# Batch 0's values pair by pair, an earlier request for w_in, and six units ahead of batch 1's scores

## The chip, the cores and the metric

The kernel runs on one core of a Trainium2 chip. The metric is device time in microseconds (us); the kernel before took 324.68 us, the median of three runs (324.43 to 324.69). Lower is better.

A core has a matrix engine (TensorE, PE in the profile, with its weight loads as PEld), three engines for elementwise work (VectorE or DVE, ScalarE or ACT, GpSimd or POOL) and SyncE (SP), which here only issues transfers. Each engine works through its own list of instructions in order; semaphores tie them together. ACT and POOL issue some transfers too.

## The reference

Attention over a sliding window with a linear bias by distance, and then a two-layer block on its output, in float32:

```python
scores = scale * np.matmul(q, k.transpose(0, 1, 3, 2))     # q, k, v: 8 batches, 8 heads, 576, 64
bias = slopes[:, None, None] * (-np.abs(rel))[None]
mask = (rel >= 0) & (rel < 128)
scores = np.where(mask, scores + bias[None], -1000000000.0)
attn = softmax(scores)                                      # over the last axis
x = np.matmul(attn, v).transpose(0, 2, 1, 3).reshape(4608, 512)
h = x @ w_in                                                # w_in: 512 x 2048
g = h * np.clip(h + 3.0, 0.0, 6.0) / 6.0
out = g @ w_out                                             # w_out: 2048 x 512
```

## The kernel before

**Tiling.** Heads go in pairs: pair g = 4·b + hp holds heads 2·hp and 2·hp+1 of batch b, so pairs 0 to 3 are batch 0, 4 to 7 batch 1, and so on to 31. The 576 positions are five blocks of 128 (the last has 64). For a pair, `scores_diag` multiplies each block of q with its own block of k and `scores_off` with the block before; `exp_diag`, `exp_off` and `exp_full` are ScalarE's exponentials, whose results wait in rooms of `w_out_sb` (batch 0) and `gbuf[1]` (batch 1). `attend`, `attend_split` or `values` multiply them with v (in `vbuf`, with a column of ones that yields the sums), and DVE divides into `avs`. `back` transposes `avs` on PE, and a copy puts the result into `xT`, the input of the second part. For pair 3 ScalarE copies the left part of `xT` (L475) and DVE the right part (L476).

**The second part.** Rows go in tiles of 512. `moe_up(nt, ms)`, a *unit* in this document, makes 128 of the 2048 hidden columns for tile nt: four matmuls (L492, one for each pair's quarter of `xT`), a ScalarE activation (L516) and a DVE multiplication (L517). Units 0 to 3 of tile 0 read w_in's first quarter, 4 to 7 the second, and so on. `up_begin` and `up_more` do the first matmuls of a unit when only some pairs are ready. `moe_down` multiplies with w_out. `fill(n)` puts the next n units or quarter-steps of `moe_down` into the engines' lists, unless the batch that they need isn't done.

**Loads.** q and k of the first batches come in four transfers each through `load_double` (two pairs at once, L98), are cast by `prepare_double` (L239, on DVE or GpSimd as the call says), transposed by nine PE transposes in a score bank and copied into `qTb` and `kTb` by `wide_double` (L282, L284). The first two pairs of batch 0 come by `load_run` (L92). v comes by `load_block` (L110): one block of 128 positions for all heads, five blocks for a batch, cast into `vbuf` by `cast_v` (L193). w_in's first quarter is loaded in float32 into `raw`, a part of `gbuf[0]` (L177), and cast by `cast_raw` (L180), one of its four pieces at a time. The other quarters come through GpSimd's own queue with a cast on the way, `load_w_in` (L169); `second_w_in` asks for the second and is held back by a one-element memset of `w_out_sb` until pair 1's exponentials in that room have been read.

**Order.** No scheduler moves anything: `manual_schedule` keeps the order of the calls as written. `first_batch` does batch 0, the start of the units and the preparation of batch 1's q and k; `second_batch` does batch 1's scores with units between; from pair 8 on `segment` repeats a fixed pattern. The PSUM banks are two wide score buffers ("sc"), two "h", one "av" and one "o"; a unit of tile 0 takes an "h" bank, but units 2, 8 and 12 take "av" and units 5 and 11 "o". A tile waits until the last reader of its bank is done.

Of the kernel before, what the change touches and what calls it, by code (L numbers as in the profile page):

```python
# [10 lines left out]
FP32 = mybir.dt.float32  # L11
BF16 = mybir.dt.bfloat16
# [6 lines left out]
def kernel(  # L19
# [88 lines left out]
    def load_block(b, nm, j, eng):  # L108
        n = min(128, S - j * 128)
        eng.dma_start(out=tokens(b, nm)[:n, j, :, :],  # L110
                      in_=src_of[nm][b, :, ds(j * 128, n), :].rearrange("h p d -> p h d"))

    def load_tokens(b, nm):
        for j in range(NQ):
            load_block(b, nm, j, nc.sync)
# [24 lines left out]
    def memsets():  # L140
        nc.gpsimd.memset(vbuf[0][:, :, :, D:W], 1.0)
        nc.gpsimd.memset(vbuf[0][64:128, 4, :, 0:D], 0.0)

    def memsets_later():
        for i in range(2):
            nc.gpsimd.memset(p4buf[i], 1.0)
        nc.gpsimd.memset(kTb[1][:, :, 4, LAST:128], 0.0)
        nc.gpsimd.memset(vbuf[1][:, :, :, D:W], 1.0)
        nc.gpsimd.memset(vbuf[1][64:128, 4, :, 0:D], 0.0)
        nc.gpsimd.memset(tbuf[64:128, :, 4, :], 0.0)  # L150

    def warm_up(n):
# [38 lines left out]
    def cast_v(b, j, copy):  # L191
        n = min(128, S - j * 128)
        copy(out=vbuf[b % 2][:n, j, :, 0:D], in_=ld[b, "v"][:n, j, :, :])  # L193

    def cast_tokens(b, nm):
        s = ld[b, nm]
# [72 lines left out]
    def double_copy(b, dp, nm, i, copies):  # L269
        dst = (qTb if nm == "q" else kTb)[b % 2][:, 2 * dp + i, :, :]  # L270
        for part, (t0, t1) in enumerate(((0, 5), (5, RT))):
            copies[part](out=dst.rearrange("p j c -> p (j c)")[:, 0:S].rearrange(
                             "p (a t) -> p a t", t=RT)[:, :, t0:t1],
                         in_=st[b, dp, nm, part].rearrange("p t (a i) -> p i a t", i=2)[:, i])
# [38 lines left out]
    def scores_diag(g):  # L313
        rooms(g)
        b, hp = divmod(g, NP)
        qT, kT = qTb[b % 2][:, hp, :, :], kTb[b % 2][:, hp, :, :]
        first = not diag_tabled(g)
        if (g, "scd") not in st:
            tables_diag(g)
        scd = st[g, "scd"]  # L320
        for j in range(4):
            for e in range(2):
                r = slice(e * D, (e + 1) * D)
                nc.tensor.matmul(scd[:, e, ts(j, 128)], lhsT=kT[r, j, :],  # L324
                                 rhs=qT[r, j, :], start=first, stop=first or j == 3)
# [40 lines left out]
    def exp_full(g):  # L366
        for e in range(2):
            exp_diag(g, e)
        exp_off_full(g)
# [89 lines left out]
    def by_xbar(g):  # L459
        return g >= XB and g not in (XB + 2, XB + 3)  # L460

    def back(g, tag=None):
        b, hp = divmod(g, NP)
        avs = st[g, "avs"].rearrange("p j e d -> p j (e d)")
        if by_xbar(g):
            nc.sync.dma_start_transpose(
                out=xT[:, hp, ds(b % 4 * S, SP)].rearrange("p (j c) -> p j c", j=NQ),
                in_=avs.rearrange("p j c -> p (j c)"))
            return
        tag = tag or ("o" if b < 2 else "h")  # L470
        tp = BANKS[tag].tile([128, SP], BF16, tag=tag, name="tb", padded_shape=[128, 1024])
        for j in range(NQ):
            nc.tensor.transpose(tp[:, ts(j, 128)], avs[:, j, :], ident)
        if g == NP - 1:
            nc.scalar.copy(out=xT[:, hp, ds(b % 4 * S, 256)], in_=tp[:, 0:256])  # L475
            nc.vector.tensor_copy(out=xT[:, hp, ds(b % 4 * S + 256, S - 256)], in_=tp[:, 256:S])  # L476
            return
        eng = nc.vector.tensor_copy if g == 2 * NP - 1 else nc.scalar.copy
        eng(out=xT[:, hp, ds(b % 4 * S, S)], in_=tp[:, 0:S])  # L479
# [123 lines left out]

    def first_batch():
        prepare(0, (V, A))
        load_block(0, "v", 1, nc.scalar)
        for j in (4, 0, 2, 3):
            load_block(0, "v", j, nc.sync)
        load_raw()
        warm_up(5)  # L610
        tables_diag(0)
        tables_off(0)
        transposes(0, (V, A))
        scores_diag(0)
        prepare(1, (P, V))
        transposes(1, (V, V))
        scores_off(0)
        exp_full(0)
        scores_diag(1)
        prepare_double(0, 1, (V, P), "qk")  # L620
        tables_off(1)
        scores_off(1)
        double_begin(0, 1, "q", ("av", "o"))
        double_begin(0, 1, "k", ("h", "h"))
        exp_full(1)
        double_copy(0, 1, "q", 0, (V, V))
        double_copy(0, 1, "k", 0, (A, A))
        scores_diag(2)
        double_copy(0, 1, "q", 1, (V, V))
        double_copy(0, 1, "k", 1, (V, V))  # L630
        tables_off(2)
        scores_off(2)
        exp_full(2)
        scores_diag(3)
        cast_v(0, 4, P)
        cast_v(0, 0, P)
        cast_v(0, 1, P)
        cast_v(0, 2, V)
        cast_v(0, 3, V)
        scores_off(3)  # L640
        exp_full(3)
        attend(0)
        for dp in range(2):
            for nm in "kq":
                load_double(1, dp, nm, nc.sync)
        load_tokens(1, "v")
        attend_split(1, ("av", "h"))
        attend(2)
        back(0, "o")
        cast_raw(0, P)  # L650
        cast_raw(1, P)
        attend(3)
        cast_raw(2, A)
        back(1, "av")
        cast_raw(3, P)
        prepare_double(1, 0, (P,), "k")
        second_w_in()
        up_begin(0, 0, 1)
        up_begin(0, 1, 1)
        back(2, "o")  # L660
        prepare_double(1, 0, (V,), "q")
        up_more(0, 0, 2)
        up_more(0, 1, 2)
        back(3, "av")
        wide_double(1, 0, "k", V)
        wide_double(1, 0, "q", A)
        up_more(0, 0, 3)
        up_more(0, 1, 3)
        done[0] = NP
        fill(2)  # L670
        prepare_double(1, 1, (P,), "k")
        load_w_in(2)
        prepare_double(1, 1, (P,), "q")
        load_w_in(3)
        for dp in range(2):
            for nm in "kq":
                load_double(2, dp, nm, nc.sync)

    def second_batch():
        scores_diag(NP + 0)  # L680
        exp_diag(NP + 0, 0)
        exp_diag(NP + 0, 1)
        fill(2)
        scores_off(NP + 0)
        exp_off_full(NP + 0)
        wide_double(1, 1, "k", V)
        fill(1)
        wide_double(1, 1, "q", V)
        fill(1)
        scores_diag(NP + 1)  # L690
        exp_diag(NP + 1, 0)
        exp_diag(NP + 1, 1)
        fill(2)
        scores_off(NP + 1)
        exp_off_full(NP + 1)
        fill(1)
        cast_tokens(1, "v")
        scores_diag(NP + 2)
        exp_diag(NP + 2, 0)
        exp_diag(NP + 2, 1)  # L700
        fill(1)
        scores_off(NP + 2)
        exp_off_full(NP + 2)
        fill(2)
        for i in range(0, 4):
            load_w_out(i)
        g = 2 * NP - 1
        scores(g)
        exp_diag(g, 0)
        exp_diag(g, 1)  # L710
        prepare_double(2, 0, (V, P))
        prepare_double(2, 1, (P, P))
        nc.gpsimd.memset(ldbuf[2][:, 0:1], 0.0)
        load_tokens(2, "v")
        for dp in range(2):
            load_double(3, dp, "k", nc.sync)
        load_tokens(3, "q")
        exp_off_full(g)
        fill(1)
        attend(NP)  # L720
        fill(1)
        attend(NP + 1)
        fill(1)
        back(NP)
        attend(NP + 2)
        fill(1)
        back(NP + 1)
        double(2, 0, "k", 0, "av", A)
        attend(NP + 3)
        back(NP + 2)  # L730
        double(2, 0, "k", 1, "av", A)
        wide_double(2, 0, "q", A)
        up_begin(1, 0, 3)
        back(2 * NP - 1)
        up_begin(1, 1, 3)
        done[0] = 2 * NP
        fill(2)
        scores_diag(2 * NP)
        scores_off(2 * NP)
# [50 lines left out]
    with tc.manual_schedule(engines=every):  # L790
        load_run(0, "k", nc.scalar)
        load_run(0, "q", nc.sync)
        load_run(1, "k", nc.scalar)
        load_run(1, "q", nc.sync)
        load_double(0, 1, "k", nc.scalar)
        load_double(0, 1, "q", nc.sync)
        constants()
        memsets()
        memsets_later()
        first_batch()  # L800
        second_batch()
        fill(2)
        segment(2 * NP, G, lambda g: FILLS.get(g, (1, 1, 1, 2, 0, 1, 2)))
        done[0] = G
        fill(len(units))
# [30 lines left out]
```

## Time and profile before

| what | value |
|---|---|
| runs | 324.43, 324.68, 324.69 us |
| span of the profiled execution, first to last instruction | 321.8 us |
| the profiled execution's own time | not listed beside its span; the runs' median is 2.9 us above the span |
| TensorE clock granted | 1.000 |
| busy: PE, DVE, ACT, POOL | 308.2, 175.5, 196.0, 138.4 us |
| transfers | 52.43 MB, 118977 of 131426 packets under 512 B |
| the chain that ended last, by engine | PE 83%, DMA 7%, ACT 4%, DVE 2%, issue 2% |

How to read it. Times in the timeline and in the chain count from the first instruction. A row of the timeline has the start, the time taken, the engine, the line of the kernel, the operation, what it writes and reads, how many were merged, and in brackets how long the engine had been idle and what released it. A row of the chain has the start, the time and what the chain ran through. A row of the windows has a stretch and its length; then for PE, PEld, DVE, ACT and POOL the busy time and the number of instructions; then the granted clock, the mean busy share of the DMA engines and GB/s.

### The profile page before, as it was taken

To read this page: it belongs to the slowest core of one execution; us is meant where nothing else is said; L and a number is where in the kernel's file an instruction comes from. 1 tells how busy PE (TensorE), PEld (TensorE's weight loads), DVE (VectorE), ACT (ScalarE), POOL (GpSimd) and SP (SyncE) were. 2 spreads that over 40 slices of the span, in tenths; PEclk is the share of its full clock that TensorE was granted. 3 is DMA by queue.
4 is the path that set the end of the run, shared out by engine and by line. 5 is a ranking of instruction groups with operands and counts; after the bars stand their busy time and mean duration, and the time that the engine had idled before them with its cause. 6 is when DMAs were issued, how large, how long until landed. Compare 5 with 4: busy or idle time off the path is not lost.

```text
span 321.8 us, 6865 instructions
## 1 busy us (share of the span) xinstructions
PE 308.2 (96%) x2620; PEld 164.6 (51%) x2659; DVE 175.5 (55%) x346; ACT 196.0 (61%) x337; POOL 138.4 (43%) x247
## 2 busy tenths in 40 slices
PE   6888999999999999999999999999999999999996
PEld 3564465455555545455667655455454444444443
DVE  6686595564346655555555556554655455445510
ACT  3857977877777766766676667666764344244401
POOL 7364590665494767446654663663331000000000
PEclk9999999999999999999999999999999999999999
DMA  7999999899999999999799999922011200000112
GB/s 273 262 369 210 269 233 214 235 200 189 201 256 170 242 200 189 204 202 230 179 214 207 211 189 202 236 66 89 20 55 59 80 34 34 33 33 35 65 49 83
DMA packets 131426, 52.43 MB, mean 163 GB/s; under 512 B 118977, under 2 KB 122817, under 8 KB 131393
## 3 DMA queue, kind: packets, MB, share of 16 engines
q1 hardware_dynamic: 125648, 46.15, 67.0%
q0 software_dynamic: 3696, 3.67, 7.0%
q10 hardware_dynamic: 2048, 2.16, 2.2%
q8 instruction: 21, 0.34, 0.5%
q14 instruction: 13, 0.10, 0.1%
HBM read 36.70 MB, written 9.44 MB: 143 GB/s over the span
## 4 chain that ended last, share of the span: by engine, by line
PE 83%; DMA 7%; ACT 4%; issue 2%; DVE 2%; POOL 1%; SPq 0%; ACTq 0%; DVEq 0%
PE ops L547 37%; PE hps L492 35%; DMA gbuf<-in_moe_w_in_dram 3%; PE scd L324 2%; DMA w_in_sb<-in_moe_w_in_dram 2%; PE av L419 2%; DMA ldbuf<-in_k_dram 2%; PE av L411 2%; ACT r L516 2%; PE sco L356 1%; PE ops L528 1%; DVE gbuf L517 1%; PE tp L254 1%; ACT gbuf L379 1%; ACT xT L479 1%
## 5 line engine op out<-in xcount | busy, mean ns | idle before, releaser
L517 DVE SCALAR_TENSOR_TENSOR gbuf<-r,hps 128x512 bf16<-128x512 f32 x144 | 98.5, 687 | 102.3 <-ACT r L516 99.4
L516 ACT ACTIVATE r<-hps,bias 128x512 f32<-128x512 f32 x144 | 98.8, 690 | 90.4 <-PE hps L492 89.3
L492 PE MATMUL hps<-xT,w_in_sb 128*128 128x512 bf16 (+1 forms) x622 | 143.3, 357 | 2.3 <-DMA w_in_sb<-in_moe_w_in_dram 0.9
L547 PE MATMUL ops<-w_out_sb,gbuf 128*128 128x512 bf16 x539 | 134.0, 379 | 2.4 <-issue 1.7
L492 PEld LDWEIGHTS <-w_in_sb 128*128 128x128 bf16 x640 | 59.0, 98 | 55.3 <-issue 1.7
L547 PEld LDWEIGHTS <-gbuf 128*128 128x128 bf16 x560 | 52.2, 98 | 56.9
L382 POOL TENSOR_SCALAR_AFFINE_SELECT pd<-pd 128x512 bf16<-128x512 bf16 x48 | 29.5, 631 | 37.8 <-ACT pd L379 37.7
L392 POOL TENSOR_SCALAR_AFFINE_SELECT po<-po 128x512 bf16<-128x512 bf16 x48 | 30.1, 633 | 32.6 <-ACT po L389 32.4
L556 DVE COPY osb<-ops 128x512 f32<-128x512 f32 x33 | 22.7, 688 | 22.0 <-PE ops L547 21.9
L379 ACT ACTIVATE pd<-scd,bias_d 128x512 bf16<-128x512 f32 x48 | 31.5, 684 | 4.7 <-PE scd L324 4.7
L389 ACT ACTIVATE po<-sco,bias_o 128x512 bf16<-128x512 f32 x48 | 33.1, 690 | 0.0
L206 POOL CAST tbuf<-ldbuf 128x512 bf16<-128x512 f32 (+1 forms) x45 | 25.5, 611 | 17.1 <-issue 17.1
L430 DVE TENSOR_TENSOR avs<-av,rc 128x384 bf16<-128x384 f32 (+1 forms) x48 | 23.6, 491 | 1.6
L419 PEld LDWEIGHTS <-pd 128*128 128x128 bf16 x192 | 14.3, 97 | 7.9 <-issue 0.5
L411 PE MATMUL av<-vbuf,po 128*128 128x65 bf16 x192 | 18.0, 193 | 0.0
L419 PE MATMUL av<-vbuf,pd 128*128 128x65 bf16 x192 | 17.3, 194 | 0.0
L411 PEld LDWEIGHTS <-po 128*128 128x128 bf16 x192 | 14.3, 98 | 2.9 <-DVE avs L430 0.5
L395 ACT ACTIVATE p4buf<-sco,bias_d 128x64 bf16<-128x64 f32 x48 | 15.6, 325 | 0.0
L199 POOL CAST vbuf<-ldbuf 128x1024 bf16<-128x1024 f32 x14 | 14.2, 1041 | 2.4 <-DMA ldbuf<-in_v_dram 2.4
L324 PEld LDWEIGHTS <-kTb 64*128 64x128 bf16 x256 | 7.3, 94 | 14.3 <-issue 10.0
L324 PE MATMUL scd<-qTb,kTb 64*128 64x128 bf16 x256 | 12.7, 219 | 1.9 <-ACT kTb L232 1.2
L239 POOL CAST pr<-ldbuf 128x576 bf16<-128x576 f32 x18 | 11.5, 671 | 2.0 <-DMA ldbuf<-in_k_dram 1.9
(107 smaller groups left out, 216.7 us busy)
## 6 DMA issues: line engine op xcount, KB each, us to landing
out_dram<-osb SPq DMA_DIRECT2D x33, 256.0 KB, 2.5
ldbuf<-in_v_dram SPq DMA_DIRECT2D x31, 256.0 KB, 5.0
ldbuf<-in_q_dram SPq DMA_DIRECT2D x20, 256.0 KB, 4.8
ldbuf<-in_k_dram SPq DMA_DIRECT2D x16, 256.0 KB, 4.6
ldbuf<-in_q_dram SPq DMA_DIRECT2D x12, 288.0 KB, 6.4
ldbuf<-in_k_dram SPq DMA_DIRECT2D x12, 288.0 KB, 6.7
w_out_sb<-in_moe_w_out_dram POOLq DMA_DIRECT2D x4, 512.0 KB, 10.0
w_in_sb<-in_moe_w_in_dram POOLq DMA_DIRECT2D x3, 512.0 KB, 8.6
```

Of the source, the lines that this page charges most:

```text
L206: nc.gpsimd.tensor_copy(out=tbuf[:m, :, j, :], in_=s[:m, j, :, :].rearrange("p (i e) d -> p i (e d)", e=2))
L324: nc.tensor.matmul(scd[:, e, ts(j, 128)], lhsT=kT[r, j, :], rhs=qT[r, j, :], start=first, stop=first or j == 3)
L379: nc.scalar.activation(out=pd[:, e, :, :].rearrange("p j c -> p (j c)"), in_=sc[:, e, :], func=ACT.Exp, bias=bias_d[:, h:h + 1], scale=scale)
L382: nc.gpsimd.affine_select(out=pd[:, e, :, :], in_=pd[:, e, :, :], pattern=[[0, 4], [1, 128]], channel_multiplier=-1, base=0, compare_op=AL ...
L389: nc.scalar.activation(out=po[:, e, :, :].rearrange("p j c -> p (j c)"), in_=sc[:, e, :], func=ACT.Exp, bias=bias_o[:, h:h + 1], scale=scale)
L392: nc.gpsimd.affine_select(out=po[:, e, :, :], in_=po[:, e, :, :], pattern=[[0, 4], [-1, 128]], channel_multiplier=1, base=-1, compare_op=A ...
L411: nc.tensor.matmul(out_av, lhsT=po[:, e, qt % 4, :], rhs=vb[:, qt - 1, h, :], start=True, stop=False)
L419: nc.tensor.matmul(out_av, lhsT=d, rhs=vb[:, qt, h, :], start=(qt == 0), stop=True)
L492: nc.tensor.matmul(hps[:, lo:hi], lhsT=w_in_sb[:, ks, ts(ms, 128)], rhs=xT[:, ks, ds(src, hi - lo)], start=(ks == 0), stop=(ks == n_ks - 1))
L516: nc.scalar.activation(out=r6, in_=hps, func=ACT.Relu, bias=bias3[:, 0:1], scale=1.0 / 6.0)
L517: nc.vector.scalar_tensor_tensor(out=gts[nt][:, ms, :], in0=r6, scalar=1.0, in1=hps, op0=ALU.min, op1=ALU.mult)
L547: nc.tensor.matmul(ops[nt, sub], lhsT=gts[nt][:, ms, ts(sub, 128)], rhs=w_out_sb[:, ms, :], start=(ms == 0), stop=(ms == n_ms - 1))
```

## The change

It is confined to the first two batches.

- v of batch 0 is loaded by heads: block 4 first, as one block, and then for each head the first 512 positions in one transfer (`load_heads`), nine transfers, all issued by SP. Before, there were five blocks, one of them issued by ACT.
- GpSimd casts all of it, one pair of heads at a time (`cast_heads`); before, DVE cast two of the five blocks.
- The values of pairs 0, 1 and 2 come by `attend_split` between the scores of pairs 2 and 3 and right behind them; pair 3 keeps `attend`. The transposes of pairs 0 and 1 in `back` use a score buffer.
- w_in's second quarter is asked for right behind these, ahead of the casts of the first quarter, and the third behind them. GpSimd now casts all four pieces of the first quarter; ScalarE cast one of them before.
- q and k of batch 1's first two pairs are cast together; their transposes (`wide_double`) come behind `fill(6)` instead of ahead of `fill(2)`, so six units stand ahead of batch 1's first scores. Four later calls of `fill(2)` become `fill(1)`.
- Some memsets change places: three of `memsets_later` go into `memsets`, the rest behind the request for the fourth quarter.

```diff
+    def load_heads(b, nm, hp, eng):
+        for e in range(2):
+            h = 2 * hp + e
+            eng.dma_start(out=tokens(b, nm)[:, 0:4, h, :],
+                          in_=src_of[nm][b, h, 0:512, :].rearrange("(j p) d -> p j d", p=128))
...
+    def cast_heads(b, hp, copy):
+        copy(out=vbuf[b % 2][:, 0:4, ds(2 * hp, 2), 0:D], in_=ld[b, "v"][:, 0:4, ds(2 * hp, 2), :])
...
     def first_batch():
         prepare(0, (V, A))
-        load_block(0, "v", 1, nc.scalar)
-        for j in (4, 0, 2, 3):
-            load_block(0, "v", j, nc.sync)
+        load_block(0, "v", 4, nc.sync)
+        for hp in range(NP):
+            load_heads(0, "v", hp, nc.sync)
         load_raw()
...
+        tables_diag(2)
+        tables_off(2)
         scores_diag(2)
         double_copy(0, 1, "q", 1, (V, V))
         double_copy(0, 1, "k", 1, (V, V))
-        tables_off(2)
         scores_off(2)
         exp_full(2)
+        cast_v(0, 4, P)
+        for hp in range(NP):
+            cast_heads(0, hp, P)
+        attend_split(0, ("av", "o"))
         scores_diag(3)
-        cast_v(0, 4, P)
-        cast_v(0, 0, P)
-        cast_v(0, 1, P)
-        cast_v(0, 2, V)
-        cast_v(0, 3, V)
+        attend_split(1, ("h", "h"))
         scores_off(3)
         exp_full(3)
-        attend(0)
         for dp in range(2):
             for nm in "kq":
                 load_double(1, dp, nm, nc.sync)
         load_tokens(1, "v")
-        attend_split(1, ("av", "h"))
-        attend(2)
-        back(0, "o")
-        cast_raw(0, P)
-        cast_raw(1, P)
+        attend_split(2, ("av", "o"))
+        pair = ps_sc.tile([128, 2, 512], FP32, tag="sc", name="backs")
+        place = [pair[:, i, :].bitcast(BF16)[:, 0:SP] for i in range(2)]
+        back(0, place=place[0])
+        back(1, place=place[1])
+        second_w_in()
+        for ks in range(n_ks):
+            cast_raw(ks, P)
+        load_w_in(2)
         attend(3)
-        cast_raw(2, A)
-        back(1, "av")
-        cast_raw(3, P)
-        prepare_double(1, 0, (P,), "k")
-        second_w_in()
+        prepare_double(1, 0, (P, V), "kq")
+        back(2, "o")
         up_begin(0, 0, 1)
         up_begin(0, 1, 1)
-        back(2, "o")
-        prepare_double(1, 0, (V,), "q")
         up_more(0, 0, 2)
         up_more(0, 1, 2)
         back(3, "av")
-        wide_double(1, 0, "k", V)
-        wide_double(1, 0, "q", A)
         up_more(0, 0, 3)
         up_more(0, 1, 3)
         done[0] = NP
-        fill(2)
+        fill(6)
+        wide_double(1, 0, "k", V)
+        wide_double(1, 0, "q", A)
+        load_w_in(3)
+        memsets_later()
         prepare_double(1, 1, (P,), "k")
-        load_w_in(2)
         prepare_double(1, 1, (P,), "q")
-        load_w_in(3)
...
     def second_batch():
         scores_diag(NP + 0)
         exp_diag(NP + 0, 0)
         exp_diag(NP + 0, 1)
-        fill(2)
+        fill(1)
         scores_off(NP + 0)
...
         scores_diag(NP + 1)
         exp_diag(NP + 1, 0)
         exp_diag(NP + 1, 1)
-        fill(2)
+        fill(1)
         scores_off(NP + 1)
...
         scores_off(NP + 2)
         exp_off_full(NP + 2)
-        fill(2)
+        fill(1)
         for i in range(0, 4):
             load_w_out(i)
```

More of the change, by code (lines that the diff above doesn't have):

```diff
@@ L142, in memsets @@
         nc.gpsimd.memset(vbuf[0][64:128, 4, :, 0:D], 0.0)
+        nc.gpsimd.memset(kTb[1][:, :, 4, LAST:128], 0.0)
+        nc.gpsimd.memset(vbuf[1][:, :, :, D:W], 1.0)
+        nc.gpsimd.memset(vbuf[1][64:128, 4, :, 0:D], 0.0)
     def memsets_later():
@@ L146, in memsets_later @@
             nc.gpsimd.memset(p4buf[i], 1.0)
-        nc.gpsimd.memset(kTb[1][:, :, 4, LAST:128], 0.0)
-        nc.gpsimd.memset(vbuf[1][:, :, :, D:W], 1.0)
-        nc.gpsimd.memset(vbuf[1][64:128, 4, :, 0:D], 0.0)
         nc.gpsimd.memset(tbuf[64:128, :, 4, :], 0.0)
@@ L460, in by_xbar, with back @@
         return g >= XB and g not in (XB + 2, XB + 3)
-    def back(g, tag=None):
+    def back(g, tag=None, place=None):
         b, hp = divmod(g, NP)
@@ L470, in back @@
         tag = tag or ("o" if b < 2 else "h")
-        tp = BANKS[tag].tile([128, SP], BF16, tag=tag, name="tb", padded_shape=[128, 1024])
+        tp = place
+        if tp is None:
+            tp = BANKS[tag].tile([128, SP], BF16, tag=tag, name="tb", padded_shape=[128, 1024])
         for j in range(NQ):
@@ L798 @@
         memsets()
-        memsets_later()
         first_batch()
```

## The prediction

> **What bounds the kernel now.** I read the page first, then the chain of waits in order of time, then the timeline around batch 0's end, then windows. The page says that TensorE (PE) is nearly always at work:
>
> ```profile
> span 321.8 us, 6865 instructions
> PE 308.2 (96%) x2620; PEld 164.6 (51%) x2659; DVE 175.5 (55%) x346; ACT 196.0 (61%) x337; POOL 138.4 (43%) x247
> ```
>
> So 13.6 us of PE idleness is all that an order can win, and the windows say where it lies: PE is busy 254.3 of the 258 us from 52 to 310, but 32.6 of the 36 from 16 to 52. A delay at 52 us is therefore paid in full at the end, and a gain there is kept in full. The chain says what the start waits for:
>
> ```profile
> 9.90 9.09 DMA gbuf<-in_moe_w_in_dram
> ...
> 20.72 1.26 POOL pr L239 x2
> 21.98 7.49 DMA w_in_sb<-in_moe_w_in_dram
> 29.47 0.05 issue
> 29.52 0.39 PE hps L492
> ```
>
> Two transfers: w_in's first quarter (raw, into gbuf), which lands at 19.00, and the second quarter, asked for at 21.98 and landed at 29.47. The timeline shows how batch 0 turns into batch 1:
>
> ```profile
> 21.55 1.40 DVE L239 CAST pr<-ldbuf 128x576 bf16<-128x576 f32 x2
> 22.87 0.31 DVE L476 COPY xT<-tb 128x320 bf16<-128x320 bf16 x1
> 23.10 1.35 DVE L284 COPY kTb<-tp 128x1152 bf16<-128x1152 bf16 x1
> 23.73 1.12 ACT L284 COPY qTb<-tp 128x1152 bf16<-128x1152 bf16 x1 [1.17 <-PE tp L282]
> 24.90 0.40 PE L324 MATMUL scd<-qTb,kTb 64*128 64x128 bf16 x8 [0.34 <-ACT qTb L284]
> 29.52 1.04 PE L492 MATMUL hps<-xT,w_in_sb 128*128 128x512 bf16 x3 [0.90 <-DMA w_in_sb<-in_moe_w_in_dram]
> 31.85 0.40 PE L324 MATMUL scd<-qTb,kTb 64*128 64x128 bf16 x8
> 35.75 0.40 PE L324 MATMUL scd<-qTb,kTb 64*128 64x128 bf16 x8
> 39.65 0.40 PE L324 MATMUL scd<-qTb,kTb 64*128 64x128 bf16 x8
> 51.58 0.40 PE L324 MATMUL scd<-qTb,kTb 64*128 64x128 bf16 x8
> ```
>
> The rows of L324 are the diagonal scores of pairs 4, 5, 6, 7 and 8: my milestones. The bracket on 29.52 is the stall that the change aims at, 0.90 us. Between milestones PE shares the pace with ScalarE:
>
> ```profile
> 36.00:38.00 2.00, 1.95 (x24) 1.03 (x20) 0.69 (x1) 2.00 (x4) 0.13 (x1) 1.00 1.10 258
> 38.00:40.00 2.00, 2.00 (x17) 0.83 (x16) 0.81 (x2) 2.00 (x4) 1.92 (x3) 1.00 1.04 369
> 40.00:42.00 2.00, 1.95 (x28) 1.14 (x28) 2.00 (x4) 2.00 (x4) 2.00 (x4) 1.00 1.06 392
> ```
>
> The fourth pair of numbers is ScalarE: 2.00 of 2.00. Exponentials that start later have no slack here.
>
> **Part 1, values of batch 0.** v's bytes stay; five loads become nine, each issue near 0.6 us (rows of 0.4 to 0.9), so SP issues some 5.4 us of them instead of 5.19 and raw's issue slips from 9.90 by about 1 us. That is hidden while DMA has v's bytes to move: I keep v's last landing at 16.3 (its load is issued at 8.52, 7.8 us to landing) and raw's at 19.0. Casts: GpSimd 0.61 each, five in all; DVE loses two of 0.43. The last ends at 16.3+0.6 = 16.9. Tables of pair 2 ahead of its scores cost the first exponential about 0.3 us; values between the scores and backs in a score bank move work that ends before 19. The memsets put off (0.74 + 0.52 on GpSimd) stand ahead of casts whose scores come after 33. All this ends at one gate: the last x slice. Its DVE half (L476) stands behind the two casts of q for batch 1, and that q lands 6.7 us after issue at 14.60 and 15.29, so at 21.3 and 22.0. Cast 22.0+0.74, copy 0.31: 23.1, as before (23.18). GpSimd now casts all of raw, 4×0.58 from 19.05 to 21.4 (before 20.8): inside the same gate. Worth of part 1: nothing, unless raw and q land sooner.
>
> **Part 2, the second quarter.** Its request waits for pair 1's values (PE, about 16) and the last cast: 16.9 instead of 21.98. Queued behind it on GpSimd are raw's casts, which wait for 19.0 anyway. When does it land? The nearest rows give 7.2 us (w_out's first part, issued at 40.73, landed near 47.9) and 7.5 us (this transfer): 24.4. Against that: before, it landed 2.5 us after the last SP load issued ahead of it (a v block, 20.52 + 6.5 = 27.0). In the new order the loads ahead of it are the first six or seven of batch 1's q and k, the seventh landing at 17.23 + 7.0 = 24.2; plus 2.5 is 26.7, one load earlier 26.0. I take 26.4, since that rule counts the queue that is really there, and keep 24.4 and 28.
>
> [...]
>
> **Part 3, six units first.** A unit (moe_up) is four matmuls, 0.86 us on PE in the chain. From 23.1: units 0 and 1 need their last slice, 0.43. Unit 3 needs unit 0's bank back: matmul 0.39 (row at 29.52), ScalarE 0.69, DVE 0.69 and hand-overs: 25.05, done 25.9. Unit 4 starts when the quarter lands, 26.4, and ends at 27.3; PE works in order, so behind this wait stand unit 5, the transposes and every score of batch 1. Unit 5 ends at 28.1. Then wide transposes of k and q (0.50 each, 30.39 to 30.89): 28.6 and 29.2. Unit 5's ScalarE and DVE steps end at 29.75, and only then DVE copies k: 29.75 + 1.35 = 31.1; ScalarE's q copy ends by 30.5. **Scores of pair 4 at 31.1 instead of 24.90: 6.2 us later**, with four more units done. PE idles 29.2 to 31.1, since no unit is left between the transposes and the scores; before, slices of units 0 and 1 covered that copy but for 0.34.
>
> **Part 4, what the later stages give back.** Before, the steps between milestones are 6.95, 3.90, 3.90 and 11.93 us with 4, 3, 3, 4 units in them; now 3, 2, 2, 3. Blocks on PE: scores 0.33, off-diagonal tables and scores 0.86 (33.92 to 34.78), wide 0.50.
> - 4 to 5: 0.33 + 3×0.86 + 0.86 + 2×0.50 = 4.8. The 0.90 stall is out of it.
> - 5 to 6, 6 to 7: PE 0.33 + 0.86 + 2×0.86 = 2.9; ScalarE two exponentials 1.14, one 0.91, two r of 0.58 (start to start) = 3.2. ScalarE decides: 3.2 each.
> - 7 to 8: four pairs' values pass DVE and ScalarE in turn (DVE without a gap from 43.13 to 49.55); a unit less gives between 0 and 0.86. I take 0: 11.9.
> Sum 23.1 against 26.68: 3.6 us back.
>
> **Sum.** 31.1 + 23.1 = 54.2 against 51.58: **2.6 us later**, carried to the end, where both orders are the same. The executed profile: 321.8 + 2.6 = 324.4. The median of the runs lies 2.9 us above the span; the same is added: 324.68 + 2.6 = **327.3 us**. Bounds: no wait for the quarter (landing by 25.9, −0.5), a unit saved in the last step (−0.86), one of the two ScalarE steps at PE's 2.9 (−0.3): 325.6. The quarter at 28 instead of 26.4, because the last head or the request is late: 328.9.
>
> **Rivals.**
> (a) *Queues share.* If the quarter's packets take turns with batch 1's loads from about 19, these run near half pace: q's second half lands near 24.5 instead of 22.0, the gate opens at 25.6, and the quarter, landed by then, no longer adds its 0.5: 2.0 us more, 329.3. For it: from 28 to 30 us, quarter and v blocks together, 201 GB/s against 391 from 18 to 20. Against: while the quarter was outstanding, the loads issued just before it still landed on pace (19.06 + 6.0, 19.77 + 6.4, 20.52 + 6.5). [...]
> (b) *Faster: v by heads runs at the pace of the large loads.* v moved at 217 to 253 GB/s (8 to 14 us), q and k at 390. A head lies in one piece in memory. At 390, v's 1.18 MB ends 2.3 us sooner, raw and q with it, the gate opens at 20.9, the scores of pair 4 come at 28.5, and with the last step a unit shorter the end is 0.9 us ahead: 323.8. It decides if pair 4's scores start before 28.5 (51.58 − 23.1). Against it: the pieces stay 256 bytes, and the page counts 118977 of 131426 packets under 512 B.
> (c) *Nothing shows.* All three lower bounds hold at once, and raw and q land 0.5 us sooner because SP no longer issues its last v load as late as 8.52 for 1.3 us: 325.6 − 0.5 = 325.1, too near to 324.68 to tell.
>
> **Chances.** Forecast 0.65 (325.6 to 328.9), (a) 0.22, (b) 0.08, (c) 0.05. A measurement of this kernel can tell about 0.2%, 0.65 us, from no change. Faster 0.08, within 0.05, slower 0.87. The range takes forecast and (a): 325.6 to 329.5.
>
> **What would show it.** Right: pair 4's scores near 31, pair 8's near 54; raw at 19; DVE's last xT copy at 23 behind the casts of q; PE idle about 2 us ahead of pair 4's scores (L334 in the new file); request of the quarter near 17. Wrong: pair 4's scores before 28.5, v landed near 14, or steps between milestones far below 3.2; (a) shows as q of batch 1 landing after 24.

## The result, and the profile after

The changed kernel takes 328.86 us, the median of four runs (328.44 to 329.50), against 324.56 (324.20 to 324.69) for the kernel before in the same comparison: a ratio of 1.014, interval 1.012 to 1.0159, so 1.4% slower. The profiled execution took 328.44 us with a span of 326.6, 4.8 us more than before. The forecast was 327.3, with a range of 325.6 to 329.5.

The page of the changed kernel, its span, the engines' busy time and the granted clock in 40 slices:

```profile
span 326.6 us, 6878 instructions
PE 308.5 (94%) x2620; PEld 164.8 (50%) x2659; DVE 175.8 (54%) x348; ACT 196.0 (60%) x336; POOL 139.9 (43%) x250
PEclk9997999999999999999999999999999999999999
```

PE has hardly more to do (308.5 against 308.2 us), so 4.5 of the 4.8 us are idle time. The 7 in the fourth slice (24.5 to 32.7 us) is new: before, the clock was whole throughout. The chain of waits, over the same stretch as before:

```profile
15.97 7.70 DMA ldbuf<-in_q_dram
23.69 0.75 DVE pr L249
24.44 0.24 DVE xT L488
24.72 5.70 PE hps L504 x18
...
31.85 1.28 DVE kTb L294
```

The chain now runs through q of batch 1 (issued at 15.97, landed at 23.66), its cast, the last x slice, eighteen unit matmuls and the copy of k to pair 4's scores. Both transfers of w_in, which carried the chain before, are gone from it. DVE and PE in the timeline (L249 was L239, L488 was L476, L294 was L284, L504 was L492, L334 was L324):

```profile
22.48 0.75 DVE L249 CAST pr<-ldbuf 128x576 bf16<-128x576 f32 x1 [1.85 <-DMA ldbuf<-in_q_dram]
23.69 0.75 DVE L249 CAST pr<-ldbuf 128x576 bf16<-128x576 f32 x1 [0.46 <-DMA ldbuf<-in_q_dram]
24.36 0.31 DVE L488 COPY xT<-tb 128x320 bf16<-128x320 bf16 x1
```

```profile
24.72 5.68 PE L504 MATMUL hps<-xT,w_in_sb 128*128 128x512 bf16 x18 [2.65 <-DVE xT L488]
33.17 0.40 PE L334 MATMUL scd<-qTb,kTb 64*128 64x128 bf16 x8 [1.76 <-DVE kTb L294]
38.08 0.40 PE L334 MATMUL scd<-qTb,kTb 64*128 64x128 bf16 x8
41.38 0.40 PE L334 MATMUL scd<-qTb,kTb 64*128 64x128 bf16 x8
44.42 0.40 PE L334 MATMUL scd<-qTb,kTb 64*128 64x128 bf16 x8
56.15 0.40 PE L334 MATMUL scd<-qTb,kTb 64*128 64x128 bf16 x8
```

The two casts of q were one row of 1.40 us before; now DVE waits for each half. PE waits 2.65 us for the slice, and the eighteen matmuls behind it take 5.68 us, 0.32 each; with the clock whole, eight of them take 1.90 us, 0.24 each (a row of experiment 2). Pair 4's scores come at 33.17 (before 24.90), pair 8's at 56.15 (before 51.58): 4.57 us later, which is nearly all of the span's 4.8. Unit 4, the first that reads the second quarter, does not wait for it: the eighteen matmuls run without a break past its landing at 27.83. The windows show what happened to the clock (PE, PEld, DVE, ACT, POOL, then the granted clock, the share of DMA and GB/s):

```profile
22.00:24.00 2.00, 0.07 (x1) 0.00 (x0) 1.07 (x2) 0.04 (x1) 2.00 (x4) 1.00 1.15 294
24.00:26.00 2.00, 1.28 (x4) 0.44 (x4) 0.67 (x2) 0.66 (x2) 1.88 (x5) 0.66 1.13 287
26.00:28.00 2.00, 2.00 (x6) 0.69 (x5) 1.28 (x2) 1.13 (x3) 0.99 (x2) 0.50 1.16 272
28.00:30.00 2.00, 2.00 (x10) 0.88 (x9) 1.25 (x2) 1.27 (x3) 0.95 (x2) 0.98 1.21 203
```

PE does next to nothing from 22 to 24, and is granted half the clock from 24.65 to 28.07. With ten matmuls in 2.00 us it is back at 0.20 each.

The question for the experiments: of 4.3 us, what do the place of the six units, the second quarter, v by heads and the clock cost? My theory was the prediction's: the place of the units costs, the early request helps, v by heads does nothing. The rivals: shared queues that hold up q, v by heads, and the clock, which had no place in the forecast.

### The profile page after: what moved, and what is told of

It reads as the page before. It is cut to its first block, busy times and chain, and to the rows that moved or that the text cites. A ratio compares the mean times of both kernels' runs of the same rounds, so it can differ in the third digit from the quotient of the medians.

```text
span 326.6 us, 6878 instructions
## 1 busy us (share of the span) xinstructions
PE 308.5 (94%) x2620; PEld 164.8 (50%) x2659; DVE 175.8 (54%) x348; ACT 196.0 (60%) x336; POOL 139.9 (43%) x250
## 4 chain that ended last, share of the span: by engine, by line
PE 83%; DMA 6%; DVE 4%; ACT 3%; issue 2%; ACTq 0%; POOL 0%; DVEq 0%; POOLq 0%
PE hps L504 36%; PE ops L559 36%; DMA ldbuf<-in_k_dram 3%; PE scd L334 2%; DMA ldbuf<-in_q_dram 2%; PE av L429 2%; PE av L421 2%; ACT r L528 2%; PE sco L366 2%; DVE gbuf L529 1%; DMA ldbuf<-in_v_dram 1%; PE ops L540 1%; DVE avs L451 1%; PE tp L264 1%; ACT gbuf L389 1%
## 5 line engine op out<-in xcount | busy, mean ns | idle before, releaser
L504 PE MATMUL hps<-xT,w_in_sb 128*128 128x512 bf16 (+1 forms) x622 | 144.5, 360 | 5.0 <-DVE xT L488 2.7
L504 PEld LDWEIGHTS <-w_in_sb 128*128 128x128 bf16 x640 | 59.5, 98 | 59.7 <-issue 6.6
L392 POOL TENSOR_SCALAR_AFFINE_SELECT pd<-pd 128x512 bf16<-128x512 bf16 x48 | 29.5, 631 | 39.3 <-ACT pd L389 39.2
L402 POOL TENSOR_SCALAR_AFFINE_SELECT po<-po 128x512 bf16<-128x512 bf16 x48 | 30.1, 632 | 32.7 <-ACT po L399 32.5
L334 PE MATMUL scd<-qTb,kTb 64*128 64x128 bf16 x256 | 12.7, 219 | 2.7 <-DVE kTb L294 1.8
L334 PEld LDWEIGHTS <-kTb 64*128 64x128 bf16 x256 | 7.2, 94 | 14.4 <-issue 9.7
L249 POOL CAST pr<-ldbuf 128x576 bf16<-128x576 f32 x18 | 11.5, 670 | 5.6 <-DMA ldbuf<-in_k_dram 4.0
```

Of the source, the lines that this page charges most:

```text
L334: nc.tensor.matmul(scd[:, e, ts(j, 128)], lhsT=kT[r, j, :], rhs=qT[r, j, :], start=first, stop=first or j == 3)
L392: nc.gpsimd.affine_select(out=pd[:, e, :, :], in_=pd[:, e, :, :], pattern=[[0, 4], [1, 128]], channel_multiplier=-1, base=0, compare_op=AL ...
L402: nc.gpsimd.affine_select(out=po[:, e, :, :], in_=po[:, e, :, :], pattern=[[0, 4], [-1, 128]], channel_multiplier=1, base=-1, compare_op=A ...
L504: nc.tensor.matmul(hps[:, lo:hi], lhsT=w_in_sb[:, ks, ts(ms, 128)], rhs=xT[:, ks, ds(src, hi - lo)], start=(ks == 0), stop=(ks == n_ks - 1))
```

## The experiments

The medians of the kernel before lie between 323.92 and 324.56 us in these comparisons; ratios are to the runs of the same comparison.

**1. The parts alone.** First the request alone, in the kernel before:

```diff
         back(0, "o")
+        second_w_in()
         cast_raw(0, P)
         cast_raw(1, P)
...
-        second_w_in()
```

> The kernel before with one edit: the request for the second quarter ahead of the casts of the first on GpSimd, so near 17.7 instead of 21.98; v, units and copies as before. Order theory (the request itself is harmless, the six units cost): the stall of 0.90 us at unit 4 is gone or short, q's casts on DVE start at most 0.5 us later, since the quarter's packets begin near 21.5, when q's first halves have landed; 0.2 to 0.8 us faster than before. Queue theory (taking turns costs more than the stall): q's second half lands after 23, the scores of pair 4 start after 26, 0.5 to 1.5 us slower.

Measured: 322.88 us, ratio 0.9966 (0.9952 to 0.998): **faster than both kernels**. The request is at 18.74, the landing at 28.01 instead of 29.47. The timeline of PE in this kernel, where unit 4 has its row at 29.31:

```profile
25.76 0.40 PE L324 MATMUL scd<-qTb,kTb 64*128 64x128 bf16 x8 [0.34 <-ACT qTb L284]
...
29.31 1.03 PE L492 MATMUL hps<-xT,w_in_sb 128*128 128x512 bf16 x3
...
31.64 0.40 PE L324 MATMUL scd<-qTb,kTb 64*128 64x128 bf16 x8
```

The bracket with 0.90 us of waiting on `w_in_sb` is gone from unit 4. In this execution the clock was at 0.50 from 7.74 to 11.15, long before the edit can act, and it runs 0.86 us behind the kernel before from the values of batch 0 (18.32 against 17.46) to pair 4's scores (25.76 against 24.90). The step to pair 5's scores then takes 5.88 us instead of 6.95, and from there on it is 0.2 us ahead (31.64 against 31.85, pair 8's scores 51.36 against 51.58). The gain of 1.1 us stands in the medians; this profile shows the wait that went, not the whole gain. q's second half landed at 21.90, on time: the packets of the quarter slow only the loads from the eighth of q and k on (25.95, and v's first blocks at 28.69 and 30.47), for which nobody waits yet.

Then v by heads alone, with its casts:

```diff
-        load_block(0, "v", 1, nc.scalar)
-        for j in (4, 0, 2, 3):
-            load_block(0, "v", j, nc.sync)
+        load_block(0, "v", 4, nc.sync)
+        for hp in range(NP):
+            load_heads(0, "v", hp, nc.sync)
...
-        cast_v(0, 0, P)
-        cast_v(0, 1, P)
-        cast_v(0, 2, V)
-        cast_v(0, 3, V)
+        for hp in range(NP):
+            cast_heads(0, hp, P)
```

> The kernel before with v loaded by heads on SP and cast by GpSimd alone, values still behind all scores. Forecast's part 1: nothing, within 0.5 us of before: raw still lands near 19, the gate stays at 23.2. Rival (b) of the prediction (heads move at the pace of the large loads): raw lands near 17, 0.5 us faster or more. Third way (four GpSimd casts in a row end later than raw's landing): values start near 17.5 instead of 16.3, up to 0.6 us slower.

Measured: 325.47 us, ratio 1.004 (1.0022 to 1.0058). v landed by 15.53 and w_in's first quarter at 18.65, both a little sooner than before, and yet q's two halves landed at 21.01 and 23.11, 2.1 us apart instead of 0.75. DVE in the timeline of this kernel:

```profile
23.13 0.75 DVE L248 CAST pr<-ldbuf 128x576 bf16<-128x576 f32 x1 [0.67 <-DMA ldbuf<-in_q_dram]
23.80 0.32 DVE L485 COPY xT<-tb 128x320 bf16<-128x320 bf16 x1
```

The slice is copied at 23.80 instead of 22.87, and pair 4's scores come at 25.82 instead of 24.90. In this profile 0.42 of the 0.92 us is left at pair 8 (52.00), since unit 4 then waits less; the medians differ by 1.35 us. "Nothing" was wrong, and the other two ways aren't seen either: w_in's first quarter did not land near 17, and the values of batch 0 are divided only 0.16 us later (17.62 against 17.46). The quarter was asked for at 21.64 here and its first packets move at 25.8, when both halves of q have landed: shared queues can't be the reason. Nor can the later issue of q (15.12 and 15.83, before 14.60 and 15.29): in the request alone it was issued at 15.16 and 15.85 and landed at 21.13 and 21.90.

And the order alone, six units first, in the kernel before:

```diff
-        wide_double(1, 0, "k", V)
-        wide_double(1, 0, "q", A)
         up_more(0, 0, 3)
         up_more(0, 1, 3)
         done[0] = NP
-        fill(2)
+        fill(6)
+        wide_double(1, 0, "k", V)
+        wide_double(1, 0, "q", A)
...
-        fill(2)
+        fill(1)
```

(the last for three calls in `second_batch`).

> The kernel before with part 3 alone: six units ahead of the wide transposes of batch 1, and four fewer units between the scores. If the units' place is what costs, by the working of the prediction's parts 3 and 4: the second quarter still lands near 29.5 us, unit 4 starts there, units 4 and 5 end at 31.2, the transposes at 32.3, the copy of k from 32.9 to 34.25, pair 4's scores near 34.3; steps after it 4.9, 3.3, 3.1 and 11.8 (23.1), so pair 8's scores near 57.4 against 51.58: 5.8 us later, some 330 us, and PE idle for about 3.5 us ahead of unit 4, behind which the clock may halve and add up to 1.7 us. The rival: the order by itself is nearly free and costs only together with the other two parts; then pair 8's scores at or before 53 and a time within 1.5 us of the kernel before.

Measured: 330.91 us, ratio 1.0202 (1.0163 to 1.0241). PE at unit 4 in this kernel:

```profile
30.04 3.60 PE L492 MATMUL hps<-xT,w_in_sb 128*128 128x512 bf16 x8 [3.26 <-DMA w_in_sb<-in_moe_w_in_dram]
```

The wait for the quarter (landed 30.00) is 3.26 us, all scores of batch 1 stand behind it, and from 28.52 on the clock is halved for 6.83 us: eight matmuls take 3.60 us. Pair 4's scores come at 36.73, 6.73 us after the landing, where the next kernel, with the clock whole, needs 4.71. The expectation had the scores near 34.3; of the 2.4 us that it missed, 2.0 are this slow clock, for which it allowed up to 1.7, and the rest is the later landing (30.00, not 29.5). The rival, that the order is nearly free, falls.

**2. Two parts at a time.** Request and order, without v by heads (the first and the third edit above):

> The kernel before with parts 2 and 3 (the early request and the six units) and without part 1 (v by heads). If part 1 adds its 1.3 us on top of whatever the other parts do: 328.9 - 1.3 = 327.5 us, with the gate (DVE's last xT copy) near 23.5, the second quarter landed near 28 and pair 4's scores near 32. If the wait of unit 4 for the second quarter covers part 1's delay: the gate earlier than in the changed kernel, but unit 4 at 28, pair 4's scores at 32.6 to 33.2 and the time within 0.6 us of 328.9.

Measured: 327.65 us, ratio 1.0111 (1.0087 to 1.0136), clock whole in all four runs. PE in the timeline of this kernel:

```profile
23.16 1.46 PE L492 MATMUL hps<-xT,w_in_sb 128*128 128x512 bf16 x6 [0.66 <-DVE xT L476]
...
27.68 1.90 PE L492 MATMUL hps<-xT,w_in_sb 128*128 128x512 bf16 x8 [1.62 <-DMA w_in_sb<-in_moe_w_in_dram]
32.35 0.40 PE L324 MATMUL scd<-qTb,kTb 64*128 64x128 bf16 x8 [1.76 <-DVE kTb L284]
```

This is the forecast's own course of things, step by step: the gate at 23.1, then a wait of unit 4 for the quarter, then scores 4.71 us after its landing (27.64). The forecast had 23.1, 26.4 and 31.1, a distance of 4.7. Only the landing was 1.2 us later. The two expectations share this result: the time is the first one's (327.5), and the place of pair 4's scores between the two, with the wait of unit 4 that the second one named.

Then the changed kernel with the old order, which is v by heads and the request together (and the changes of place in batch 0):

```diff
+        wide_double(1, 0, "k", V)
+        wide_double(1, 0, "q", A)
         up_more(0, 0, 3)
         up_more(0, 1, 3)
         done[0] = NP
-        fill(6)
-        wide_double(1, 0, "k", V)
-        wide_double(1, 0, "q", A)
+        fill(2)
...
-        fill(1)
+        fill(2)
```

> The changed kernel with the old place of the units: k and q of batch 1 are transposed ahead of the last slices, two units first, and the old numbers of units between batch 1's scores; v by heads, the early request and the casts stay as changed. Order theory (six units ahead of the scores cost by themselves what the forecast's parts 3 and 4 say, and what stands in front only adds to it): pair 4's scores come near 26 instead of 33.2, the stall at unit 4 is gone or short, and the time falls by 3.5 to 4.5 us to 324.4 to 325.4. Rival (the early request is what costs, since it halves the pace of batch 1's loads): the time stays within 1.5 us of the changed kernel's, 327.4 or more.

Measured: 325.65 us, ratio 1.0044 (1.0018 to 1.007). Pair 4's scores come at 27.61 and pair 8's at 53.58. Here the place of the units is thus worth 1.014 − 1.0044 = 0.0096, or 3.1 us, a little less than the order theory's 3.5 to 4.5. Without part 1 the same step costs 1.0111 − 0.9966 = 0.0145, or 4.7 us, and alone 2.0%, or 6.5 us: it has no single price, since what it adds depends on which wait stands in front. What is left, 1.4 us, stands against −1.1 us (−0.34%) for the request alone: v by heads, with the changes of place in batch 0, takes back its gain and more. The changes of place were not run by themselves. PE in the timeline of this kernel, at the units behind the gate:

```profile
25.77 1.91 PE L504 MATMUL hps<-xT,w_in_sb 128*128 128x512 bf16 x4
```

Four matmuls in 1.91 us, against 1.03 at the whole clock (the last kernel of experiment 3): the clock was halved here as well, from 25.31 to 28.72, after PE had idled 2.19 us.

**3. The clock and the gate, in the changed kernel.** Twelve multiplications by the identity into a free score buffer, whose results nobody reads, keep PE at work while it waits for the slice:

```diff
         up_more(0, 1, 3)
+        filler = ps_sc.tile([128, 2, 512], FP32, tag="sc", name="filler")
+        for i in range(12):
+            nc.tensor.matmul(filler[:, i % 2, :].rearrange("p (j c) -> p j c", j=4), lhsT=ident,
+                             rhs=ident.rearrange("p (j c) -> p j c", j=1).to_broadcast([128, 4, 128]),
+                             start=True, stop=True)
         done[0] = NP
         fill(6)
```

> The changed kernel with twelve matmuls of the identity (512 columns, results unused) on PE between the third slices of units 0 and 1 and the fourth, where the trace has PE idle for 2.65 us and the granted clock at 0.5 from 24.65 to 28.07. Clock theory (the idle time halves the clock for 3.4 us, which costs half of that): the clock stays at 1.00, unit 5 ends 1.7 us sooner, the time falls by 1.2 to 1.7 us, less if unit 4 then waits for the second quarter, which lands at 27.83. Rival (the slow matmuls wait for banks or weights, and the clock is only a sign): no change, within 0.3 us, or slower by the added matmuls.

Measured: 328.23 us, ratio 1.0125 (1.009 to 1.016), clock 0.999 over the profile's span and 1.00 from 20 to 30 us. PE in the timeline of this kernel:

```profile
24.80 1.46 PE L504 MATMUL hps<-xT,w_in_sb 128*128 128x512 bf16 x6 [0.16 <-POOL p4buf L156]
...
28.30 1.90 PE L504 MATMUL hps<-xT,w_in_sb 128*128 128x512 bf16 x8 [0.60 <-DMA w_in_sb<-in_moe_w_in_dram]
32.97 0.40 PE L334 MATMUL scd<-qTb,kTb 64*128 64x128 bf16 x8 [1.76 <-DVE kTb L294]
```

The first units run at full pace, and then unit 4 waits 0.60 us for the quarter, which landed at 28.25. Scores come 0.2 us sooner than in the changed kernel. The 1.2 to 1.7 us did not come back: the ratios differ by 0.0015, some 0.5 us, which their intervals don't tell from nothing. The quarter had been hidden behind the slow clock; taking away the one shows the other.

The gate instead: the casts of q behind the copy of the slice on DVE, so that the slice does not wait for q.

```diff
-        prepare_double(1, 0, (P, V), "kq")
+        prepare_double(1, 0, (P,), "k")
...
         back(3, "av")
+        prepare_double(1, 0, (V,), "q")
```

> The changed kernel with the two DVE casts of q for batch 1 behind the copy of pair 3's right half into xT instead of ahead of it. Gate theory (that copy waits for q's landing at 22.38 and 23.66 through DVE's order): the copy starts near 21.7, units 0 to 3 run from 22.0 to 25.2 at full clock, then unit 4 waits for the second quarter near 27.8; pair 4's scores at 32.5 instead of 33.2, time 0.5 to 1.0 us shorter. Rival (the gate decides all that follows): the whole 2.7 us between 22.0 and 24.7 and the 1.7 us of slow clock come back, 4 us shorter.

Measured: 329.95 us, ratio 1.0164 (1.0115 to 1.0213). The slice is copied at 21.71, 2.65 us sooner, and pair 4's scores come at 33.93, 0.76 us later. PE at unit 4 in this kernel:

```profile
27.98 3.17 PE L504 MATMUL hps<-xT,w_in_sb 128*128 128x512 bf16 x8 [2.30 <-DMA w_in_sb<-in_moe_w_in_dram]
```

PE now idles 2.30 us in front of the quarter, and the halved clock (28.45 to 31.86) falls on the units behind it. The expected 0.5 to 1.0 us did not come: opening the first gate gains nothing while the second stays shut.

The request late again, behind w_in's first quarter and the casts of k, all else as changed:

```diff
-        second_w_in()
         for ks in range(n_ks):
             cast_raw(ks, P)
-        load_w_in(2)
         attend(3)
         prepare_double(1, 0, (P, V), "kq")
+        second_w_in()
+        load_w_in(2)
```

> The changed kernel with the request for the second quarter behind the casts of the first and of k for batch 1, as before the change, and the third quarter right behind it; the six units still first. Queue theory (the quarter's packets take turns with batch 1's loads and halve their pace): q lands 0.75 us apart again, its second half near 22.3 instead of 23.7, the gate opens near 23.3, the clock stays at 1.00 there; the quarter lands at 29 to 31, units 4 and 5 wait for it, pair 4's scores at 33 to 35. Time within 1.5 us of the changed kernel's, either way. Rival (q is late because v and raw are): q's second half still lands after 23.4.

Measured: 332.71 us, ratio 1.0261 (1.023 to 1.0292). The quarter lands at 30.76, PE idles 3.77 us, the clock is halved for 6.83 us, and pair 4's scores come at 37.53. That is 1.2%, or 3.9 us, above the changed kernel, where 1.5 us was expected at most: the wait was foreseen, the slow clock behind it was not. The later loads of q and k are 0.75 us apart again (23.08, 23.83, 24.58, 25.33) instead of 1.5: it is the quarter's packets that stretched them. But a jump is left ahead of q's first half (20.62 to 22.32).

And the clock in the old order: ten identity multiplications, as above, in experiment 2's second kernel.

> The changed kernel with the old place of the units (the first experiment), and ten matmuls of the identity, results unused, where PE idles for 2.19 us between the transposes of pair 3 and those of k. Clock theory: the granted clock stays at 1.00 where it was 0.5 from 25.31 to 28.72, pair 4's scores at 26.3 to 26.8 instead of 27.6, and 0.5 to 1.5 us come back, which leaves 0 to 0.9 us over the kernel before. Rival (the old order's remaining loss is all in the late landing of q): no change within 0.4 us.

Measured: 325.59 us, ratio 1.0035 (1.0009 to 1.006). The clock was whole, pair 4's scores came at 26.11 instead of 27.61, and the median is the same as without them (325.65). What the slow clock costs in the time isn't settled: ten runs of the kernel without the filler hold two with the clock at 1.000 and spans of 321.7 and 323.0, where the other eight have 323.5 to 325.8; yet the nine runs with the filler have spans from 322.1 to 325.7.

**4. What holds up q when v comes by heads.** In the changed kernel and the six above with v by heads one jump of 1.3 to 2.1 us stands between two landings of batch 1's first q and k, where 0.75 is the rule. Each time a packet of 16 KB on the queue of instructions, which takes about 1 us (0.94 from 19.34 on in the changed kernel, 1.08 from 20.44 on in the kernel before), begins 0 to 1.3 us ahead of the first of the two landings. Of the four kernels with v in blocks only the order alone has such a jump (21.81 to 23.16, packet at 21.1), behind q, where nobody waits; in the kernel before, the packet at 20.4 does no harm. To move the packet, 28 small multiplications (32 columns, results unread) stand at the start of v by heads alone:

```diff
+    def warm_small(n):
+        w = ps_av.tile([128, 4, 128], FP32, tag="av", name="w2")
+        for _ in range(n):
+            nc.tensor.matmul(w[:, 0, 0:32], lhsT=ident, rhs=ident[:, 0:32], start=True, stop=True)
...
         warm_up(5)
+        warm_small(28)
```

> v by heads alone, with 28 small matmuls of 32 columns more at the start, whose results nobody reads: they move the fetch of PE's instructions, a packet of 16 KB of about 1 us on one of the DMA queues, from 21.0 us to some 2 to 3 us earlier, and keep PE about 0.5 to 1 us longer at the start, where it waits anyway. If that packet is what holds up the second half of q of batch 1 (landed 23.11, 2.1 us behind the first half, with v by heads alone): q's second half 0.75 us behind the first again, near 21.8, pair 4's scores near 25.0 and a time within 0.5 us of the kernel before (ratio 1.000 to 1.002). If the order and size of v's loads are what holds it up: the jump of 1.4 us or more stays near the same transfer, and the ratio stays near 1.004. If the jump moves to another transfer with the packet, the packet is at work.

Measured: the packet moved from 21.0 to 19.3, and the jump moved with it, from q's second half (21.01 to 23.11) to k's (19.84 to 21.60). The time stayed: 325.47 us, ratio 1.0036 (1.002 to 1.0052), since what lands behind the jump is late all the same: q's second half again at 23.11, the slice at 23.80, pair 4's scores at 25.83. The jump follows the packet, so the packet is at work in it; it isn't enough by itself, since with v in blocks it mostly does no harm. Why is open; the trace doesn't say which DMA engine carries it.

## Why the prediction was right, and where it was not

The sign and the range held, and so did the cause: six units ahead of batch 1's scores cost more than the earlier request gains. The wait that stands in front was not the forecast's. It had unit 4 wait for the second quarter; in the changed kernel the last x slice waits for q, and the quarter has landed when unit 4 comes. That is rival (a)'s path, with q's second half at 23.66 and the gate at 24.67, where (a) had some 24.5 and 25.6. The forecast's path appears where part 1 is left out (1.62 us of waiting) and where the filler keeps the clock whole (0.60 us). The time came out 1.6 us above the forecast (328.86 against 327.3), 2.0 us by pair 8's scores (56.15 against 54.2); it lies at the forecast's upper bound of 328.9 and nearer to (a)'s 329.3, so the number alone does not choose between them. That the two paths end so close together (pair 4's scores at 33.17 behind q, at 32.97 behind the quarter with the filler) is luck.

- **Part 1, "nothing": wrong.** v's last landing (15.7, forecast 16.3), the last cast (16.4 against 16.9) and the landing of w_in's first quarter (19.5 against 19.0) were near. SP's nine issues, though, took 8.6 us (4.62 to 13.25) and not 5.4, so that w_in's first quarter was issued at 13.29, 3.4 us later than before and not 1; all but 0.5 us of this stayed hidden, as forecast. But alone the part costs 0.4%, through a step that the forecast took over from the kernel before: q "lands 6.7 us after issue". Here it took 7.2 and 7.7 us for the two halves. The second landed at 23.66, 1.67 us later than before (21.99): 0.5 us is the later landing of w_in's first quarter, 0.7 the jump (20.22 to 21.64 instead of 0.75 us), and 0.5 the step from q's first half to its second (1.28 instead of 0.75), where the second quarter's packets share the way. The gate of 23.1 became 24.67. Without part 1 and with the early request it was 23.11: without part 1 the request does not delay it.
- **Part 2, landing of the quarter at 26.4: 1.4 us too early.** The request came at 16.39 (forecast 16.9), but its 1 KB packets moved only from about 20.6 on, at some 93 KB per us beside some 195 for q and k. It landed at 27.83, inside the bound of 28. The bound for the late case was right, the rule for the middle was not.
- **Part 3, scores 4.7 us after the landing: right**, in the kernel without part 1 (4.71) and in the one with the filler (4.72). With the landing at 27.83 it gives 27.83 + 4.7 = 32.5. Measured were 33.17: the remaining 0.6 is the late gate with the halved clock behind it, a term that the forecast lacked. It had PE's idle time at the gate and took the clock of the kernel before, 1.000, for granted.
- **Part 4, steps of 4.8, 3.2, 3.2 and 11.9: right**, measured 4.91, 3.30, 3.04 and 11.73, a sum of 23.0 against 23.1. The choice to give the last step nothing back for the unit less was nearly right (0.2). Three calls of `fill(2)` become `fill(1)`, not four as the list of changes has it; the last step has a unit less because tile 0 has only 16 units.
- **The sum.** 1.4 for the landing and 0.6 for gate and clock, less 0.1 for the steps, make the 1.9 to 2.0 us at pair 8. The kernel with request and order, without part 1, is the forecast's own case, since it took part 1 for nothing: pair 8's scores come there at 55.34, 3.8 us later than before, where the forecast's 2.6 and 1.2 for the later landing make 3.8. The landing is the term that the forecast had too small.
- **Rival (a), shared queues:** half right. The loads do run at half pace: from q's second half on the trace after has landings at 23.66, 25.21, 26.70, 28.16 and 29.66, about 1.5 us apart, against 0.75 in the kernel before. But that alone delays nothing that is waited for: with the request and without part 1 q's second half landed at 21.90 and 21.92. It takes the lateness of part 1 to push q into the shared stretch. The forecast's evidence against this rival was thin: in the kernel before, the quarter's packets began only at 24.8, so that the loads that landed "on pace" by 27.0 were nearly through (28 KB per us of SP's packets from 25 to 27, 242 from 23 to 25).
- **Rival (b), v faster by heads:** v's last landing came 0.6 us sooner (15.7 against 16.3), not 2.3, and the gate opened later, not sooner. Rival (c), nothing to be seen at 325.1, is out by 3.8 us.
- **The clock, which was no rival.** Each halved stretch inside these kernels lasted 3.41 us or twice that. PE need not be idle for as long ahead of it: in the 3.41 us ahead of a halving (I took the halved stretch's own length; which length counts isn't shown) it was busy for 0.83 us in the changed kernel, 1.07 in the old order, 1.12 with q behind, 1.26 in the order alone and 0.74 with the late request; two stretches of that length, one behind the other, with 1.79 and 1.65 us of work (request and order, from 25.91) kept the clock whole. Nor does the length of the gap decide: 2.65, 2.30 and 2.19 us of idle PE brought the halving, 1.62 and 1.92 us did not (request and order; late request, ahead of its first units), and yet near the start of the request alone it came behind a gap of 1.38 us, with 1.74 us of work in the 3.41 us ahead. Where the limit lies, these traces don't say.

Of the whole: the early request alone is worth −0.34%, v by heads alone +0.40%, six units first alone +2.0%, request and units +1.1%, all three +1.4%. The request repairs a part of what the order breaks, and keeps its gain only where the order stays. The parts do not add up, since one's wait hides another's. The best version found is the kernel before with the early request and nothing else, 322.88 us.

## What to carry to other kernels

An engine that works in order waits with its whole list (in the order alone all scores of batch 1 stood behind the 3.26 us that PE waited for the quarter): filler work that needs a transfer of its own must not stand ahead of the work on the critical path, however much of it there is to fill. When two gates are late together, taking one away shows the other; so price each gate from its own release, and test a change of several parts part by part: here one part gained 0.34% and was hidden under two that lost more. Before an idle stretch of PE is called harmless, ask what it does to the clock: in the changed kernel the clock was at 0.50 for 3.41 us from the end of 2.65 us of idle PE on.

## What the runs showed of the hardware

- In the profiled executions the granted clock fell to 0.50 around idle gaps of PE of 2.19 to 3.77 us and stayed there for 3.41 us, or 6.83 around the two longest gaps (3.26 and 3.77 us). A gap of 1.92 us left it whole, and one of 1.38 us near the start of the request alone did not. At 0.50 eight matmuls took 3.60 us, at 1.00 they took 1.90. One run in four of the order alone and one in four with q behind have a mean clock of 1.000: not every execution showed the halving.
- The load of w_in's second quarter on GpSimd's queue, with a cast on the way, took 11.4 us beside the loads of SP in the changed kernel (27.83 − 16.39), 7.5 us in the kernel before, where it was asked for later: asking 5.6 us sooner brought the landing 1.6 us forward.
- Where a packet of 16 KB of instructions began 0 to 1.3 us ahead of a landing and v came by heads, the next landing was 0.6 to 1.4 us later than the usual 0.75 us; moving the packet by 1.8 us moved the jump to another transfer. In three of four kernels with v in blocks no jump went with it.
